# Attention scores in one burst over eight PSUM banks: one burst per pair, values per quad, FFN units in one stretch

## The chip, the cores and the metric

The kernel runs on one core of one Trainium2 chip. The metric is device time in microseconds, from runs of the whole kernel; lower is better. Before the change it takes 300.81 us (median of three runs, 300.67 to 305.9).

The engines are called by these names: PE (TensorE, the matrix multiplier), DVE (VectorE), ACT (ScalarE), POOL (GpSimd), SP (SyncE, which issues most DMAs). PSUM, into which PE writes its results, has eight banks of 512 fp32 columns on 128 partitions.

## What is computed

Attention with a causal mask over 576 tokens and 16 extra "beacon" keys that every query sees, for 8 batches of 8 heads of width 64; then a feed-forward layer (FFN) with the maximum of three projections over all 8 x 576 = 4608 tokens.

```python
k_all = np.concatenate([beacon_k, k], axis=2)          # (8, 8, 592, 64)
v_all = np.concatenate([beacon_v, v], axis=2)
scores = scale * np.matmul(q, k_all.transpose(0, 1, 3, 2))
scores = np.where(causal, -1000000000.0, scores)
a = np.exp(scores - scores.max(-1, keepdims=True))
a /= a.sum(-1, keepdims=True) + 1e-09
x = np.matmul(a, v_all)          # then (8, 576, 512) -> (4608, 512)
h = np.maximum(np.maximum(x @ w1, x @ w2), x @ w3)      # 512 -> 768
out = h @ w_out                                         # 768 -> 512
```

## The kernel before

Work is cut into *pairs* of heads (32: four per batch, numbered 0 to 31) and *quads* of two pairs (16). Keys of a pair lie in five tiles of 128 rows (the last has 80); tile t is needed by the queries from `q_min[t]` on (0, 112, 240, 368, 496). Everything is issued in an order written out by hand (`emit_all`, L834, under `manual_schedule`); no planner reorders it, and each engine runs its own list in order.

*Scores* (`emit_scores`, L438 to L460). The 1664 columns of a pair are split into four *groups* (`groups_any`, L69) of at most 512 columns. For each group PE multiplies the two heads of the pair side by side (64 rows of the array each) into two PSUM banks, one for each head (L450), and one ACT instruction exponentiates both into `at_sb` (L459). The pool `sc_psum` holds two such pairs of banks. POOL then zeroes the masked triangles (`emit_masks`, L478).

*Values* (`emit_pv`, L502 to L535). For a quad, four heads run side by side, 32 columns of the array each. Three parts are summed over the key tiles: a row of ones (the sums of the softmax), the even and the odd columns of V (L522). It is done in two halves of 288 queries, with two banks of the pool `pv_psum`. `invert_sums` (L538) takes Ln of the sums and Exp of minus that on ACT (L542, L544); `multiply` (L549, L554) has DVE multiply the values, read from PSUM, by it into `xT`, which holds four batches.

*FFN units*. A unit of `mm1_unit` (L572) is four matmuls of 512 columns (L582) into a bank of `ffn_psum` and one DVE copy (L590) or maximum (L592) into `hT`; one of `mm2_unit` (L613) is six matmuls (L618) and a DVE copy to `y` (L626), stored by SP (L652). A block of 512 tokens has 18 and 4 of them; there are nine blocks. `emit_ffn` (L674) emits the next unit if the running quota (`allowed`) and the finished batches (`ready`) permit.

*The order, from pair 4 on* (L844 to L893). Each pair has two steps of two groups: scores, masks, a half value pass of an earlier quad (in the first step), then FFN units and the other work of the step, with quota left over emitted at its end. "Turning" a pair is the transposing of its q and k by PE (L345) into PSUM and the copies to `qT` (ACT, L381) and `kT` (DVE, L392); it is done for pairs up to 15, one pair ahead. Pairs from 16 on are instead cast to bf16 by POOL (L218), stored to DRAM (L330) and fetched back by transposing DMAs (L337, L338), planned by `at_step` with pairs of lead. V is cast by POOL (L261). Loads are issued on SP as staging buffers come free.

*The end* (L895 to L908): the last quad's two halves between FFN units, and then FFN units alone, with the copies of the first projection given to ACT (`alone`) and banks taken from `ffn_psum` and `sc_psum` in turn.

Of the kernel before, what the change touches and what calls it, by code (L numbers as in the profile page):

```python
# [16 lines left out]
def kernel(  # L17
# [64 lines left out]

    def groups(p):
        return groups_0 if p < PPB else groups_any
# [8 lines left out]
    assert AT_W == g_base(PPB, NG)  # L93
    assert max(g_width(p, gi) for p in (0, PPB) for gi in range(NG)) <= 512
# [19 lines left out]
    at_pool = ctx.enter_context(tc.tile_pool(name="at", bufs=5))  # L114
    nrm_pool = ctx.enter_context(tc.tile_pool(name="nrm", bufs=2))
    ffn_h = ctx.enter_context(tc.tile_pool(name="ffn_h", bufs=2))
    ffn_y = ctx.enter_context(tc.tile_pool(name="ffn_y", bufs=5))
    sc_psum = ctx.enter_context(tc.tile_pool(name="sc_psum", bufs=2, space=PSUM))
    pv_psum = ctx.enter_context(tc.tile_pool(name="pv_psum", bufs=1, space=PSUM))
    dram_pool = ctx.enter_context(tc.tile_pool(name="dram", bufs=B - B_PE, space=bass.MemoryType.DRAM))  # L120
    ffn_psum = ctx.enter_context(tc.tile_pool(name="ffn_psum", bufs=2, space=PSUM))
# [32 lines left out]
    def pv_bank(i, shape, dtype):  # L154
        return pv_psum.tile(shape, dtype, name=f"pv{i}")
# [143 lines left out]
    def turn_beacons(b0, b1, src):  # L299
        n = Nb * (b1 - b0)  # L300
        ps = sc_psum.tile([128, PPB, n], BF16, name="sc")
        for pi in range(PPB):
            nc.tensor.transpose(
                ps[:, pi],
                src[:, 2 * pi : 2 * pi + 2].rearrange("p h d -> p (h d)"),
                ident[0:n, 0:n],
            )
        if b0 == 0:
            by_act(kTs[0][:, 0:Nb], ps[:, 0, 0:Nb])
        by_act(bT[:, :, Nb * b0 : Nb * b1], ps)  # L310
# [45 lines left out]
    def turn_half(p, h, pv, q_copy=None, idle=0):  # L356
        for i in range(2):
            src = stage.pop(("half16", p, h, i))
            if pv:
                bank = pv_bank(i, [128, 1024], BF16)  # L360
            else:
                bank = ffn_psum.tile([128, 1024], BF16, name="fps")
# [34 lines left out]
    def turn_apart(p, i):  # L397
        ps = ffn_psum.tile([128, S], BF16, name="fps")
        turn(p, i, ps)
        (evac_q, evac_k)[i](p, ps, by_dve)  # L400
        if i == 1:
            place_beacons(p, by_dve)

    def turn_pair(p, q_copy, shared=True):
        if shared:
            ps = sc_psum.tile([128, 2, 1024], BF16, name="sc")
            banks = [ps[:, i, 0:S] for i in range(2)]
        else:
            banks = [pv_bank(i, [128, 1024], BF16)[:, 0:S] for i in range(2)]
        for i in range(2):  # L410
            turn(p, i, banks[i])
        evac_k(p, banks[1], by_dve)
        evac_q(p, banks[0], q_copy)

    def keep_busy(n, cols=320, ffn=False):
        ps = ffn_psum.tile([128, 512], FP32, name="fps") if ffn else pv_bank(1, [128, 512], FP32)
# [23 lines left out]
    def emit_scores(p, gi):  # L440
# [4 lines left out]
        ps = sc_psum.tile([128, 2, 512], FP32, name="sc")  # L445
# [15 lines left out]
        )  # L461

# [35 lines left out]
    def emit_pv(quad, hf, first=0, last=len(passes), apart=False):  # L498
# [4 lines left out]
        if first == 0:  # L503
            if apart:
                banks = [ffn_psum.tile([128, 512], FP32, name="fps") for _ in range(2)]
            else:
                banks = [pv_bank(i, [128, 512], FP32) for i in range(2)]
# [27 lines left out]

    def invert_sums():
# [4 lines left out]
        lnd = nrm_pool.tile([128, HALF], FP32, name="lnd")  # L541
        nc.scalar.activation(out=lnd, in_=ps[0][:, 0:HALF], func=AF.Ln)  # L542
        recip = nrm_pool.tile([128, HALF], FP32, name="recip")
        nc.scalar.activation(out=recip, in_=lnd, func=AF.Exp, scale=-1.0)  # L544
# [26 lines left out]
    alone = [False]  # L571

    def mm1_unit(tb, ft, i, pool, name):
        if tb not in hTs:
            hTs[tb] = ffn_h.tile([128, n_ft, TOKB], BF16, name="hT")
        h = hTs[tb][:, ft]
        ps = pool.tile([128, TOKB], FP32, name=name)
        c0 = tb * TOKB % (RING * S)
        n0 = min(TOKB, RING * S - c0)
        for x0, o0, n in ((c0, 0, n0), (0, n0, TOKB - n0)):  # L580
            for ct in range(n_ct if n > 0 else 0):
                nc.tensor.matmul(  # L582
                    ps[:, o0 : o0 + n],
                    w_in[i][:, ct, 128 * ft : 128 * (ft + 1)],
                    xT[:, ct, x0 : x0 + n],
# [3 lines left out]
        if i == 0:  # L589
            (by_act if alone[0] else by_dve)(h, ps)  # L590
        else:
            nc.vector.tensor_max(h, h, ps)  # L592

    def mm1_halves(tb, ft, i, lo, hi, pool, name):
# [3 lines left out]
        ps = pool.tile([128, 2, MID], FP32, name=name)  # L598
# [14 lines left out]
    def mm2_unit(tb, tt, pool, name):  # L613
        hT = hTs[tb]
        c0 = tb * TOKB + 128 * tt
        ps = pool.tile([128, d_model], FP32, name=name)
        for ft in range(n_ft):
            nc.tensor.matmul(  # L618
                ps,
                hT[:, ft, 128 * tt : 128 * (tt + 1)],  # L620
                w_out_sb[:, ft, :],
                start=(ft == 0),
                stop=(ft == n_ft - 1),
            )
        y = ffn_y.tile([128, d_model], FP32, name="y")
        nc.vector.tensor_copy(y, ps)  # L626
        y_out.append((c0, y))

    def mm2_last(tb, tt, cuts):
# [3 lines left out]
        for i in range(len(cuts) - 1):  # L633
            lo, hi = cuts[i : i + 2]
            pool, name = ((ffn_psum, "fps"), (sc_psum, "sc"))[i % 2]
            ps = pool.tile([128, hi - lo], FP32, name=name)
# [33 lines left out]
    UPB = len(units) // n_tokb  # L670
    END = len(units)
    done = [0]

    def emit_ffn(limit, pool=None, name="fps"):  # L674
        if done[0] == len(units):
            return False
        need, fn, args = units[done[0]]
        if done[0] + 1 <= limit + 1e-6 and need <= ready[0]:
            fn(*args, pool or ffn_psum, name)
            done[0] += 1  # L680
            return True
        return False
# [136 lines left out]
    for quad in range(2, NPAIR // 2 - 1):  # L819
        at_pv(2 * quad + 2, 0, quad, 0)  # L820
        at_pv(2 * quad + 3, 0, quad, 1)
# [12 lines left out]
    def emit_all():  # L834
# [9 lines left out]
        for p in range(PPB, NPAIR):  # L844
            b, pi = divmod(p, PPB)
            turned = p + 1 < B_PE * PPB
            for s, gs in enumerate(steps(p)):
# [9 lines left out]
                if n_step <= N_FIRST:  # L857
                    allowed = first + n_step * (UPB - first) / N_FIRST
                else:
                    allowed = UPB + (n_step - N_FIRST) * UPB / (2 * PPB)  # L860
                if s == 0:
                    if p < PPB + 2:
                        turn_pair(p + 1, by_act, False)
                        emit_ffn(allowed)
                    elif p % 2 == 0:
                        emit_ffn(allowed)
                    if turned and p >= PPB + 2:
                        turn_pair(p + 1, by_act)
                    if p % 2 == 1 and p >= PPB + 2:
                        emit_ffn(allowed)  # L870
                    if turned:
                        place_beacons(p + 1, by_act)
# [4 lines left out]
                    emit_ffn(allowed, *(() if turned else (sc_psum, "sc")))  # L877
# [3 lines left out]
                else:  # L881
# [6 lines left out]
                    emit_ffn(allowed, *((sc_psum, "sc") if done[0] + 2 <= allowed else ()))  # L888
# [3 lines left out]
            if pi == 1 and b > 0:  # L892
                v_tiles.pop(b - 1)  # L893
        assert not plan and not loads and not pv_at
        for hf in range(2):  # L895
            multiply()
            emit_ffn(END)
            emit_ffn(END)
            emit_pv(NPAIR // 2 - 1, hf)
            finish_pv()  # L900
        store_y(len(y_out))
        alone[0] = True
        i = 0
        tail = [(ffn_psum, "fps"), (sc_psum, "sc")]
        while done[0] < END - 1 and emit_ffn(END, *tail[i % 2]):
            i += 1
# [35 lines left out]
```

## Time and profile before

| What | Before |
|---|---|
| Runs (median of three; lowest, highest) | 300.81 us (300.67, 305.9) |
| Span of the profiled execution | 299.3 us |
| Mean granted TensorE clock | 1.000 |
| PE busy | 282.3 us, 94% |
| DVE, ACT, POOL busy | 173.6, 145.8, 127.8 us |
| Exponentials (L459), 128 of them | 103.8 us |
| DMA moved | 50.68 MB |

The profiled execution's own total is not given apart from its span; the median of the runs is 1.5 us above the span.

The page of the profile gives, for each engine, busy time and its share of the span; then the span in 40 slices, each digit the busy share of a slice in tenths (PEclk is the clock granted to PE, in tenths of full). A line of a group of instructions reads: line of the kernel, engine, operation, output<-inputs, shapes, count, then busy time and mean length in ns, then the idle time of the engine just before these instructions and what ended it. A line of the timeline reads: start, length, engine, line, what, and how many; equal instructions that follow each other are merged. A line of the waits reads: who waited <- for whom: time in all, times, longest. Matmul ends are modelled, and a few matmul records are missing, so starts are the better measure on PE.

### The profile page before, as it was taken

What the parts mean: (1) busy time and instruction counts of PE and PEld (TensorE: products, weight loads), DVE (VectorE), ACT (ScalarE), POOL (GpSimd) and SP (SyncE); (2) the same over time, 40 slices, a digit from 0 to 9 for tenths busy, and PEclk for the clock granted to TensorE, in tenths of its full rate; (3) what the DMA queues carried; (4) which work ended last, traced back from release to release, by engine and by line L of the source; (5) the groups of instructions that cost most, each with busy time, mean ns of one, the idle gap of its engine ahead of it and who ended that gap; (6) DMA issues with size and microseconds to landing.
All of it is one profiled execution on the core that took longest, in us unless ns stands there. A gap on an engine that the chain in (4) does not pass through costs nothing.

```text
span 299.3 us, 8656 instructions
## 1 busy us (share of the span) xinstructions
PE 282.3 (94%) x3569; PEld 152.8 (51%) x3599; DVE 173.6 (58%) x346; ACT 145.8 (49%) x233; POOL 127.8 (43%) x253
## 2 busy tenths in 40 slices
PE   7879887999999999999999999999999999999994
PEld 4546654554545454454545777545454554444442
DVE  3756744555767575646563756375736575274372
ACT  3685484875665465546453646364636421401300
POOL 7181776666475674456455635552333210000000
PEclk9999999999999999999999999999999999999999
DMA  8989999999999999899989999894111002103003
GB/s 147 197 161 235 226 211 265 239 224 296 241 268 209 200 289 220 168 189 330 231 165 204 287 260 189 144 257 103 42 72 70 2 2 85 57 1 140 2 0 142
DMA packets 85320, 50.68 MB, mean 169 GB/s; under 512 B 64416, under 2 KB 80032, under 8 KB 85280
## 3 DMA queue, kind: packets, MB, share of 16 engines
q1 hardware_dynamic: 80672, 45.76, 67.4%
q0 software_dynamic: 4048, 4.03, 8.2%
q8 instruction: 28, 0.46, 0.7%
q10 hardware_dynamic: 560, 0.33, 0.5%
q14 instruction: 12, 0.10, 0.1%
HBM read 35.13 MB, written 14.22 MB: 165 GB/s over the span
## 4 chain that ended last, share of the span: by engine, by line
PE 81%; DMA 7%; SPq 4%; DVE 2%; ACT 2%; issue 1%; POOL 1%; POOLq 0%; DVEq 0%
PE fps L582 31%; PE sc L582 12%; PE pv L522 11%; PE fps L618 11%; PE sc L450 8%; DMA st<-in_k_dram 4%; PE sc L618 4%; SPq L245 3%; DMA quad<-in_k_dram 3%; PE sc L345 2%; ACT at_sb L459 1%; DVE xT L554 1%; POOL quad L209 1%; DVE y L626 1%; PE fps L522 0%
## 5 line engine op out<-in xcount | busy, mean ns | idle before, releaser
L459 ACT ACTIVATE at_sb<-sc 128x928 bf16<-128x928 f32 (+5 forms) x128 | 103.8, 861 | 85.2 <-PE sc L450 84.7
L582 PE MATMUL fps<-xT,w_sb 128*128 128x512 bf16 (+1 forms) x464 | 106.4, 356 | 2.1 <-issue 0.8
L478 POOL TENSOR_SCALAR_AFFINE_SELECT at_sb<-at_sb 128x256 bf16<-128x256 bf16 (+2 forms) x148 | 53.8, 382 | 99.0 <-ACT at_sb L459 98.8
L582 PEld LDWEIGHTS <-w_sb 128*128 128x128 bf16 x672 | 61.7, 98 | 65.2 <-issue 12.2
L592 DVE TENSOR_TENSOR hT<-hT,fps 128x512 bf16<-128x512 bf16 x70 | 48.0, 687 | 29.4 <-PE fps L582 29.1
L218 POOL CAST p<-st 96x768 bf16<-96x768 f32 x56 | 44.6, 822 | 1.0 <-DMA st<-in_k_dram 0.5
L582 PE MATMUL sc<-xT,w_sb 128*128 128x512 bf16 (+1 forms) x187 | 42.9, 356 | 0.1
L450 PE MATMUL sc<-qT,kT 64*128 64x288 bf16 (+5 forms) x400 | 36.0, 277 | 2.8 <-ACT at_sb L459 1.9
L618 PE MATMUL fps<-w_out_sb,hT 128*128 128x512 bf16 x143 | 34.6, 379 | 0.9 <-issue 0.6
L618 PEld LDWEIGHTS <-hT 128*128 128x128 bf16 x210 | 19.8, 98 | 24.1 <-DVE hT L592 2.1
L592 DVE TENSOR_TENSOR hT<-hT,sc 128x512 bf16<-128x512 bf16 x32 | 22.0, 688 | 16.9 <-PE sc L582 11.3
L626 DVE COPY y<-fps 128x512 f32<-128x512 f32 x25 | 17.3, 692 | 23.5 <-PE fps L618 23.5
L590 DVE CAST hT<-fps 128x512 bf16<-128x512 f32 x32 | 22.1, 692 | 12.3 <-PE fps L582 12.2
L554 DVE TENSOR_TENSOR xT<-pv,recip 128x288 bf16<-128x288 f32 (+2 forms) x93 | 27.3, 349 | 2.7 <-ACT recip L544 2.7
L522 PE MATMUL pv<-at_sb,v_sb 128*32 128x288 bf16 (+5 forms) x1376 | 28.7, 229 | 0.0
L450 PEld LDWEIGHTS <-kT 64*128 64x128 bf16 x400 | 14.3, 94 | 27.2 <-issue 21.8
L522 PEld LDWEIGHTS <-v_sb 128*32 128x32 bf16 (+1 forms) x1408 | 24.4, 96 | 1.9 <-issue 0.6
L261 POOL CAST v_sb<-st 128x1536 bf16<-128x1536 f32 (+2 forms) x21 | 18.4, 893 | 1.8 <-DMA st<-in_v_dram 1.8
L522 PE MATMUL pv<-at_sb,ones 128*32 128x288 bf16 (+4 forms) x500 | 17.4, 256 | 1.3 <-POOL at_sb L478 1.2
L542 ACT ACTIVATE lnd<-pv 128x288 f32<-128x288 f32 x31 | 12.9, 417 | 8.9 <-PE pv L522 8.9
L522 PEld LDWEIGHTS <-ones 128*32 128x32 bf16 (+2 forms) x512 | 10.9, 95 | 8.7 <-issue 6.7
L590 ACT CAST hT<-sc 128x512 bf16<-128x512 f32 x6 | 3.5, 585 | 23.7 <-PE sc L582 23.7
(74 smaller groups left out, 161.7 us busy)
## 6 DMA issues: line engine op xcount, KB each, us to landing
out_dram<-y SPq DMA_DIRECT2D x35, 256.0 KB, 3.5
st<-in_q_dram SPq DMA_DIRECT2D x28, 288.0 KB, 5.6
st<-in_k_dram SPq DMA_DIRECT2D x28, 288.0 KB, 6.2
st<-in_v_dram SPq DMA_DIRECT2D x24, 256.0 KB, 6.0
w_sb<-in_moe_w_dram POOLq DMA_DIRECT2D x6, 384.0 KB, 7.2
q_dram<-p SPq DMA_DIRECT2D x16, 144.0 KB, 2.4
k_dram<-p SPq DMA_DIRECT2D x16, 144.0 KB, 2.9
st<-in_v_dram SPq DMA_DIRECT2D x8, 224.0 KB, 6.1
```

Source lines behind the costliest of these rows:

```text
L218: cast(t16.rearrange("p r h d -> p h r d"), st[0:QP, i * NQ2 : (i + 1) * NQ2].rearrange("p (h r d) -> p h r d", h=2, r=QR),)
L261: cast(v_sb[0:n, t:t1].rearrange("p t h d -> p (t h d)"), st[0:n, (t - t_lo) * H * D : (t1 - t_lo) * H * D],)
L450: nc.tensor.matmul(ps[:, e, off : off + q1 - q0], kT[hs, 128 * t : 128 * t + 128], qT[hs, q0:q1], start=True, stop=True, tile_position=(64 ...
L459: nc.scalar.activation(out=both_heads(p, gi), in_=ps[:, :, 0 : g_width(p, gi)], func=AF.Exp, scale=scale)
L478: nc.gpsimd.affine_select(out=view, in_=view, compare_op=ALU.is_ge, fill=0.0, base=x0, pattern=[[0, 2], [1, hi - lo]], channel_multiplier=-1,)
L522: nc.tensor.matmul(ps[bank][32 * j : 32 * j + 32, lo + q0 - qa : lo + qb - qa], lhsT, at_view(PPQ * quad + j // 2, t, j % 2, q0, qb), star ...
L554: nc.vector.tensor_mul(xT[:, 2 * g + part - 1, c0 + ca : c0 + cb], ps[bank][:, lo : lo + cb - ca], recip[:, ca:cb],)
L582: nc.tensor.matmul(ps[:, o0 : o0 + n], w_in[i][:, ct, 128 * ft : 128 * (ft + 1)], xT[:, ct, x0 : x0 + n], start=(ct == 0), stop=(ct == n_c ...
L590: (by_act if alone[0] else by_dve)(h, ps)
L592: nc.vector.tensor_max(h, h, ps)
L618: nc.tensor.matmul(ps, hT[:, ft, 128 * tt : 128 * (tt + 1)], w_out_sb[:, ft, :], start=(ft == 0), stop=(ft == n_ft - 1),)
L626: nc.vector.tensor_copy(y, ps)
```

## The change

Three things change from pair 8 on (`FIRST_BURST`, batch 2), and PSUM is one tile of eight banks, `acc`, instead of three pools. For the pairs before, `Banks` hands out fixed banks as the pools did.

- *One score burst per pair*: the four groups, cut anew (`groups_whole`, from pair 6 on), are multiplied one after another into eight banks that are handed out in turn (`next_bank`); each group's exponential reads its two banks in one strided view. The cut has groups of 208, 464, 496 and 496 columns for each head.
- *One value burst per quad*: `emit_pv_whole` takes all 576 queries at once, 496 of them in one bank for each of the three parts and the last 80 of all three in a fourth bank, directly after the burst of the next even pair. ACT copies the values to SBUF (`raw`), then does Ln and Exp; DVE multiplies `raw` by the result at the end of the pair (`finish`).
- *FFN units of a pair in one stretch*, each in the next bank in turn; the last unit of a stretch is done in two halves of 256 columns in two banks (`close`). Turning comes after the first unit, planned work after the second and at the end.

`at_pool` has 4 buffers instead of 5. The pairs 4 to 7 keep their order, but no longer take FFN banks from the score pool, and pair 6 turns before its first FFN unit. At the end, the last quad's values come in one burst after three FFN units, all banks go in turn, and DVE does the copies that ACT did (`alone` is gone).

```diff
+    groups_whole = [
+        [(3, q_min[3], S)],
+        [(1, q_min[1], S)],
+        [(0, 0, TAIL)],
+        [(2, q_min[2], S), (0, TAIL, S), (4, q_min[4], S)],
+    ]
...
-    at_pool = ctx.enter_context(tc.tile_pool(name="at", bufs=5))
+    at_pool = ctx.enter_context(tc.tile_pool(name="at", bufs=4))
...
+    acc = psum.tile([128, N_BANK, 512], FP32, name="acc")
...
+    free_banks = list(range(N_BANK))
+
+    def next_bank():
+        i = free_banks.pop(0)
+        free_banks.append(i)
+        return i
...
+    def emit_burst(p):
+        at[p] = at_pool.tile([128, AT_W], BF16, name="at_sb")
+        for gi in range(NG):
+            lo, hi = sorted(next_bank() for _ in range(2))
+            off = 0
+            for t, q0, q1 in groups(p)[gi]:
+                for e in range(2):
+                    score(p, t, e, q0, q1, acc[:, (lo, hi)[e], off : off + q1 - q0])
+                off += q1 - q0
+            nc.scalar.activation(
+                out=both_heads(p, gi),
+                in_=acc[:, lo : hi + 1 : hi - lo, 0 : g_width(p, gi)],
+                func=AF.Exp,
+                scale=scale,
+            )
...
+    def emit_pv_whole(quad):
...
+        banks = [next_bank() for _ in range(4)]
+        runs = [(part, banks[part], 0, 0, TAIL) for part in range(3)]
+        runs += [(part, banks[3], part * WT, TAIL, S) for part in range(3)]
...
+        raw = pv_pool.tile([128, 2, S], FP32, name="raw")
+        for part in (1, 2):
+            nc.scalar.copy(raw[:, part - 1, 0:TAIL], acc[:, banks[part], 0:TAIL])
+        nc.scalar.copy(
+            raw[:, :, TAIL:S],
+            acc[:, banks[3], WT : 3 * WT].rearrange("p (i c) -> p i c", i=2),
+        )
+        recip = nrm_pool.tile([128, S], FP32, name="recip")
+        nc.scalar.activation(out=recip[:, 0:TAIL], in_=acc[:, banks[0], 0:TAIL], func=AF.Ln)
+        nc.scalar.activation(out=recip[:, TAIL:S], in_=acc[:, banks[3], 0:WT], func=AF.Ln)
+        nc.scalar.activation(out=recip, in_=recip, func=AF.Exp, scale=-1.0)
+
+        def finish():
+            c0 = b % RING * S
+            for i in range(2):
+                nc.vector.tensor_mul(xT[:, 2 * g + i, c0 : c0 + S], raw[:, i], recip)
...
+        for p in range(FIRST_BURST, NPAIR):
+            b, pi = divmod(p, PPB)
+            emit_burst(p)
+            finish = emit_pv_whole(p // 2 - 1) if p % 2 == 0 else None
+            for gi in range(NG):
+                emit_masks(p, gi)
...
+            while may_emit(allowed):
+                n_y = len(y_out)
+                emit_ffn(allowed, next_psum, not may_emit(allowed, 1))
+                store_y(n_y)
+                n += 1
+                if n == 1 and p + 1 < B_PE * PPB:
+                    turn_pair(p + 1, by_act, "any")
+                    place_beacons(p + 1, by_act)
+                if n == 2:
+                    for fn in plan.pop((p, 0), ()):
+                        fn()
+            if finish:
+                finish()
+            for s in range(2):
+                for fn in plan.pop((p, s), ()):
+                    fn()
```

## The prediction

> **What bounds the kernel now.** Read the page first: span, busy shares, slices.
>
> ```profile
> span 299.3 us, 8656 instructions
> PE 282.3 (94%) x3569; PEld 152.8 (51%) x3599; DVE 173.6 (58%) x346; ACT 145.8 (49%) x233; POOL 127.8 (43%) x253
> PE   7879887999999999999999999999999999999994
> PEclk9999999999999999999999999999999999999999
> ```
>
> TensorE (PE) is the bound: after slice 8 (60 us) it is full, at full clock, while VectorE (DVE), ScalarE (ACT) and GpSimd (POOL) have half their time free. Next, the table of waits: of what PE waits for, the largest is
>
> ```profile
> PE sc L450 <- ACT at_sb L459: 1.9, 5, 0.9
> ```
>
> and the five fall before 60 us. So where the change starts (pair 8, 64.3 us), PE has no waits to lose; a gain must come out of its own stream, and any wait added is paid in full. The PE timeline of a pair late in the kernel:
>
> ```profile
> 195.68 1.03 PE L582 MATMUL fps<-xT,w_sb 128*128 128x512 bf16 x4
> 196.64 0.54 PE L450 MATMUL sc<-qT,kT 64*128 64x288 bf16 x8
> 197.12 0.40 PE L522 MATMUL pv<-at_sb,ones 128*32 128x288 bf16 x12
> 197.35 0.62 PE L522 MATMUL pv<-at_sb,v_sb 128*32 128x288 bf16 x32
> 198.78 1.03 PE L582 MATMUL sc<-xT,w_sb 128*128 128x512 bf16 x4
> 199.64 1.03 PE L582 MATMUL fps<-xT,w_sb 128*128 128x512 bf16 x4
> 200.60 0.51 PE L450 MATMUL sc<-qT,kT 64*128 64x464 bf16 x4
> 201.05 1.04 PE L582 MATMUL fps<-xT,w_sb 128*128 128x512 bf16 x4
> ```
>
> Starts count, not durations (each includes some 165 ns of pipeline that the next matmul overlaps). An FFN unit of four 512-column matmuls takes 199.64 − 198.78 = 0.86 us, 216 ns a matmul, 0.42 ns a column. From 195.68, four such end at 196.54, but the scores start at 196.64: 0.10 is lost. From 200.60, 464 + 336 columns (two heads side by side) are 0.34, but the FFN starts 0.45 later: 0.11 lost. The starts of single matmuls between 60 and 245 us give the loss at each change of tile shape with hardly any scatter: 96 ns FFN to scores, 92 scores to FFN, 90 scores to values, 96 values to FFN. That is what the change can save.
>
> Last, the exponentials, by form and from the ACT timeline:
>
> ```profile
> L459 ACT ACTIVATE at_sb<-sc 128x992 bf16<-128x992 f32 x32 | 31.9, 997 | 36.5 <-PE sc L450 35.9 <-POOL at_sb L478 0.5
> L459 ACT ACTIVATE at_sb<-sc 128x928 bf16<-128x928 f32 x28 | 26.4, 944 | 45.2 <-PE sc L450 45.2
> L459 ACT ACTIVATE at_sb<-sc 128x672 bf16<-128x672 f32 x28 | 20.3, 726 | 0.0
> 56.78 3.16 ACT L459 ACTIVATE at_sb<-sc 128x928 bf16<-128x928 f32 x4 [0.50 <-PE sc L450]
> ```
>
> Four in a row, one pair's worth, take 3.16 us, while a pair's score matmuls take 0.7. Today a step's scores are followed by work in other banks, and no one waits for the exponentials.
>
> **The change, part by part.** Sums are against the profiled execution (span 299.3); the median of the runs, 300.81, lies 1.5 above it (launch and end), which I add back.
>
> *Removed: changes of shape.* Pairs 8 to 31 are 24. Before, each has two score steps (48 entries, 48 exits) and one half value pass with an exit of its own (24); the last quad's two halves add 4: 124. After: 24 + 24 + 12 + 2 = 62. Saved 62 × 94 ns = **−5.8 us**. The columns stay: scores 1664 a pair both ways; value burst, from starts of groups of four (288: 122 ns, 192: 82, 96: 42, 80: 40, 48: 27), 2.18 us a quad before in 120 matmuls and 2.20 after in 108: +0.3 in all.
>
> *Added: waits of PE for exponentials.* A burst takes banks in turn from eight, in pairs, one pair a group, and goes round all eight. One exponential reads both banks of its group as a strided view `acc[:, lo : hi+1 : hi-lo]`. If a burst starts at an even bank the groups are (0,1), (2,3).. If it starts at an odd bank, one group is (7,0), sorted to lo 0, hi 7. The view touches two banks, but its first and last address enclose all eight, and in the built program the next write of *any* bank waits for that exponential. An example from the built order is pair 13, where the banks run 3,4 / 5,6 / 7,0 / 1,2: the 496 columns go to banks 0 and 7, and the first write of bank 1 then carries a wait for ScalarE, at the count of the exponential of banks 0 and 7:
>
> ```
> L510 Matmult acc_90<-qT1_109,kT1_115 128x496
> L510 Matmult acc_90<-qT1_109,kT1_115 128x336 [waits Activation_49]
> ```
>
> Start banks follow from the counts (8 for scores, 4 for values on even pairs, one per FFN unit and one more for the split last one, 2 for a turn). Odd starts: pairs 10, 17, 22 (bank 1: group 3 wraps), 13, 14, 21, 26 (bank 3: group 2), 25, 30 (bank 5: group 1), 18, 29 (bank 7: group 0). Eleven of 24.
>
> Price, from the burst's first score: group 0 is 208 columns wide, so its exponential (416 elements, 0.51 by the slope 997 to 726 over 320 elements, 0.85 ns each) starts at about 0.32 and ends at 0.83; each later one adds its length less 0.105 of overlap (3.16 against 3.45 summed): ends 0.83, 1.67, 2.56, 3.45. PE resumes 52 ns after the exponential that it waits for (51 to 52 ns at each of the five waits above, by single starts). Unhindered, PE would start group 1 at 0.09, group 2 at 0.30, group 3 at 0.51, the next kind of work at 0.82. So wrap at group 3: 3.50 − 0.82 = 2.69, three times 8.1; group 2: 2.61 − 0.51 = 2.10, four times 8.4; group 1: 1.72 − 0.30 = 1.43, twice 2.9; group 0: 0.88 − 0.09 = 0.79, twice 1.6. Sum **+20.9 us**, nothing else on PE being late enough to absorb it. Bounds: 0, if they were all hidden; 27 if ScalarE began each chain 0.5 later. I take the worked value, for ScalarE is idle at a burst's start (below). Behind the waiting matmul stand all of PE's queue: the rest of the burst, the value burst, the FFN; DVE's evictions and POOL's masks follow late but are not the bound.
>
> *Ordinary bursts (13).* The next work takes group 0's banks: 0.88 against 0.82, 0.06 each; group 3's second bank waits for the last half eviction about as long, and the two overlap: **+0.9**.
>
> *Split last unit.* Eight 256-column matmuls (109 ns by starts) for four of 216: +8 ns, 24 times, +0.2. Where that unit is the first output unit right after the last maximum (pairs 12, 16, 20, 24, 28), its sixth matmul comes at 0.55, and the eviction that it needs ends at 0.19 + 0.69 + 0.05 = 0.93: 0.39 × 5 = **+1.9**. Bounds 0 and 3.
>
> *ScalarE copies values, VectorE multiplies from SBUF.* Per quad ACT gains copies of 496 twice (0.57 each, between 585 for 512 and 425 for 320) and 160 (0.3), and has Ln 0.59 + 0.24 and Exp 0.69 for four of 0.42 to 0.44. In an even pair that ends with the copy of qT (0.64) near 6.6, the pair is over 8.5 long: hidden, and free at the next burst. The sums' bank comes free at 5.1 against an FFN unit that wants it at 5.5: hidden by 0.4; without this cover, 0.5 × 12 = 6. DVE: 576 columns from SBUF, no row; from 450 at 288 and 248 at 96, 0.75, twice per quad; DVE has 42% free, and they run behind the pair's last eviction, before the next pair's first unit ends. Hidden.
>
> *Moved: casts, stores, fetches.* Per pair two pair casts on POOL, two stores and two transposing fetches on SP, and per batch the three V casts and the loads that they release, go behind the pair's second FFN unit or its end. A fetch lands 3 to 5 us after issue and is used over two pairs (16 us) later, on SP's queue behind output stores that wait only for an earlier unit. POOL takes masks first, then casts. The second V cast is now needed with the first value tiles: after masks (to 4.5), cast 1.46, pair casts 1.6 and 0.6 it is done near 8.2 after the odd pair's burst; the burst needs it near 8.3. Value 0, bounds 0 and 6 × 0.7. Pairs 4 to 7 lose the spare score banks for FFN units, and pair 6 turns before its unit: 0, bounds ±1. At the end VectorE takes ScalarE's 12 copies (692 ns each, unit 0.86): hidden.
>
> Sum: 299.3 − 5.8 + 0.3 + 20.9 + 0.9 + 0.2 + 1.9 = 317.7; plus 1.5: **319 us**, 6% slower.
>
> **Rivals.** (1) *Not slower*: the wrapped waits cost nothing because the exponentials are done when PE arrives. Then 319.2 − 20.9 = 298.3. It decides if the eleven waits come to under 2.5 us in all (8.5 for less than 2% slower); for it speaks only ScalarE's 51% idle time, against it that a pair's exponentials cannot finish before 3.1 us after its scores began. Chance 0.08; a further 0.02 for this without the smaller costs (295.0) and with some saving that I do not see, below 294.8. (2) *ScalarE or the V cast is late*, so each chain begins some 0.25 later: 24 × 0.25 = 6, **325**. For: in even pairs with a turn ScalarE's list ends only 2 us before the burst. Against: 2 us is spare. 0.14. (3) *The clock falls in the gaps.* The profile never shows it below full in gaps up to 1.2 us; it fell 4.1 us after the last matmul (295.2 to 299.3), and the start took 4.4 us at half speed. Up to 2.2 us lost in each of the three long waits: **326**. The gaps of 2.7 are nearer to the 4.1 that drops it than to 1.2, but short of it: 0.05. (4) *The wrapped waits are shorter*, say group 3's and 2's cut by a third through earlier starts: 319 − 5.5 = 313.5. 0.08.
>
> On rival 3: the Trainium skill, "TensorE: Matmul & The Clock Gate", section "Why this matters for your kernels", asks for no idle gaps over about 3 us between bursts of matmuls, since the clock then halves. By it the 2.7 us gaps still pass and the sum stays; a longer one would not. The trace agrees as far as it goes: full clock through every gap below 1.2 us, and a drop after 4.1.
>
> **How the numbers follow.** Forecast 319 (0.63); rivals 0.10, 0.14, 0.05, 0.08. Range 310 to 326: rival 4 and a cheaper chain below, rivals 2 and 3 above; rival 1 is left out. Within 2% of 300.8 (what a measurement here tells from no change) lie 294.8 to 306.8: rival 1 but for its 0.02. Faster 0.02, same 0.08, slower 0.90.
>
> **What would show it.** In the profile after: PE waits for the exponential's line from score lines, value lines and FFN lines, eleven times 0.8 to 2.7 us, some 21 us in all, at pairs 10, 13, 14, 17, 18, 21, 22, 25, 26, 29, 30, and nothing longer than 0.1 at the others; PE busy share down to about 89%; 62 fewer shape changes. Wrong if those waits are absent, or if PE waits for VectorE, POOL or a DMA instead.

## The result, and the profile after

The changed kernel takes 326.07 us (median of 4 runs, 325.05 to 328.76) against 303.36 for the kernel before (4 runs, 300.67 to 307.42) beside it: 1.0806 times the time, 95% interval 1.0711 to 1.0901. It is slower by about 8%. 319.0 was forecast, with a range of 310 to 326: the sign was right, and the time lies just above the range. Medians here are of all runs, while ratios and their intervals leave out the runs in a slower state, which the kernel before and most others show now and then. The profiled execution of the changed kernel took 325.05 us, with a span of 323.3.

The page of the profile after, with the span, the busy shares, the slices of TensorE (PE) and of its clock, and the groups of the exponentials and of the new operations:

```profile
span 323.3 us, 8611 instructions
PE 288.2 (89%) x3539; PEld 165.1 (51%) x3539; DVE 182.0 (56%) x330; ACT 150.0 (46%) x247; POOL 132.9 (41%) x253
PE   7789969996997979968997889987998899999995
PEclk9999989997999899979998999999999999999999
L528 ACT ACTIVATE at_sb<-acc 128x416 bf16<-128x416 f32 (+1 forms) x96 | 76.1, 867 | 87.1 <-PE acc L510 56.1
L651 DVE TENSOR_TENSOR xT<-raw,recip 128x576 bf16<-128x576 f32 x26 | 20.7, 838 | 0.0
```

PE falls from 94% to 89% of the span, and its row now has sixes, sevens and eights where it was all nines from 60 us on. The row below it is the one to look at a second time: the clock, all nines before, now dips five times. Nothing else is nearer to its limit than it was.

The table of waits of the changed kernel (who waited <- for whom: time in all, times, longest):

```profile
PE acc L510 <- ACT at_sb L528: 12.5, 8, 2.0
PE acc L628 <- ACT at_sb L528: 5.0, 2, 2.5
PE acc L750 <- ACT at_sb L528: 2.6, 1, 2.6
...
PE acc L750 <- DVE hT L722: 1.4, 5, 0.3
```

Eight, two and one: the eleven waits for ScalarE (ACT), met by score lines (L510), by value lines (L628) and by an FFN line (L750), as forecast. By the starts of single matmuls they are 2.60, 2.72 and 2.68 us at pairs 10, 17 and 22, 2.14 or 2.15 at 13, 14, 21 and 26, 1.46 and 1.47 at 25 and 30, 1.18 and 1.12 at 18 and 29: 21.8, or 21.5 without the change of shape (some 93 ns) that the first three contain. PE resumes 51 to 54 ns after the exponential's end. One more wait, of 0.77 us, falls on pair 8 itself, whose first burst waits for pair 7's last exponential; the kernel before lost 0.39 and 0.18 in that pair.

One of them, and what follows it, in the PE timeline of the changed kernel (pair 17: 12 score matmuls from 138.11, then FFN), and in its table of stretches (us; busy time and instructions of each engine; then granted clock, DMA share, GB/s):

```profile
138.11 0.97 PE L510 MATMUL acc<-qT,kT 64*128 64x208 bf16 x12
141.65 4.65 PE L750 MATMUL acc<-w_out_sb,hT 128*128 128x512 bf16 x13 [2.56 <-ACT at_sb L528]
```

```profile
135.00:138.45 3.45, 3.16 (x25) 1.77 (x24) 2.50 (x5) 0.00 (x0) 0.00 (x0) 1.00 1.02 133
138.45:141.86 3.41, 0.85 (x11) 0.47 (x8) 1.73 (x3) 3.13 (x4) 1.66 (x4) 1.00 0.70 171
141.86:145.27 3.41, 3.41 (x10) 1.17 (x9) 0.69 (x1) 0.00 (x0) 3.41 (x6) 0.50 0.64 171
145.27:148.70 3.43, 3.43 (x20) 1.84 (x19) 1.80 (x3) 0.00 (x0) 1.14 (x3) 1.00 0.80 239
```

In the second stretch PE is busy for 0.85 of 3.41 us; in the third the granted clock is 0.50, and in the fourth it is 1.00 again. So the wait is paid twice: once as a gap, and once at half speed behind it. From pair 8 on there are four such stretches, at 77.01, 104.32, 141.86 and 176.00 us, each 3.413 long, and all whole multiples of 3.413 apart. A stretch of 3.413 at half speed does 1.71 less of work: 6.8 us in all, in this execution. The other three runs had mean clocks of 0.968, 0.973 and 0.951 against its 0.973, so the number of falls is not the same in each.

**Where the time went.** The stretch from the first score of pair 8 to PE's last matmul is the measure for all that follows: 237.2 us in the kernel before (57.79 to 294.99), 260.7 after, 23.5 longer. What lies before pair 8 (the head) differs between executions of one kernel: pair 8 begins at 59.8 us in one profile of e2 below and at 62.9 in the other.

| term | us |
|---|---|
| eleven waits for the exponentials | +21.5 |
| four stretches at half clock | +6.8 |
| second-product halves waiting for hT, 0.40 once and 0.46 four times | +2.2 |
| last group's second bank (below, e8 and e9), and the split unit | +2.3 |
| pair 8's own burst, 0.77 against 0.39 and 0.18 | +0.2 |
| 62 fewer changes of shape at 94 ns | -5.8 |
| small stalls of the kernel before that are gone (hT 0.41, three of 0.33 for xT, some 1.3 in the FFN) | about -2.7 |
| sum / measured | 24.5 / 23.5 |

The 1.0 us between sum and measurement is not assigned.

### The profile page after: what moved, and what is told of

Same layout as the page of the kernel before. It is cut to its first block, busy times and chain, and to the rows that moved or that the text cites. A ratio compares the mean times of both kernels' runs of the same rounds, so it can differ in the third digit from the quotient of the medians.

```text
span 323.3 us, 8611 instructions
## 1 busy us (share of the span) xinstructions
PE 288.2 (89%) x3539; PEld 165.1 (51%) x3539; DVE 182.0 (56%) x330; ACT 150.0 (46%) x247; POOL 132.9 (41%) x253
## 4 chain that ended last, share of the span: by engine, by line
PE 73%; ACT 9%; DMA 6%; POOL 4%; issue 3%; DVE 3%; SPq 1%; ACTq 0%; POOLq 0%; DVEq 0%
PE acc L703 39%; PE acc L750 13%; PE acc L628 10%; ACT at_sb L528 7%; PE acc L510 5%; DMA st<-in_v_dram 3%; DMA quad<-in_k_dram 2%; ACT at_sb L504 2%; POOL v_sb L303 2%; PE acc L387 1%; PE acc L594 1%; DVE hT L722 1%; POOL p L260 1%; PE acc L495 1%; SPq L222 1%
## 5 line engine op out<-in xcount | busy, mean ns | idle before, releaser
L703 PE MATMUL acc<-xT,w_sb 128*128 128x512 bf16 (+1 forms) x732 | 136.5, 342 | 0.0
L528 ACT ACTIVATE at_sb<-acc 128x416 bf16<-128x416 f32 (+1 forms) x96 | 76.1, 867 | 87.1 <-PE acc L510 56.1
L703 PEld LDWEIGHTS <-w_sb 128*128 128x128 bf16 x732 | 69.8, 98 | 57.8 <-issue 0.8
L722 DVE TENSOR_TENSOR hT<-hT,acc 128x512 bf16<-128x512 bf16 (+1 forms) x114 | 69.8, 630 | 38.7 <-PE acc L703 36.1
L750 PE MATMUL acc<-w_out_sb,hT 128*128 128x512 bf16 (+1 forms) x246 | 53.4, 369 | 4.0 <-ACT at_sb L528 2.6
L720 DVE CAST hT<-acc 128x512 bf16<-128x512 f32 (+1 forms) x54 | 33.0, 630 | 41.5 <-PE acc L703 35.3
L757 DVE COPY y<-acc 128x512 f32<-128x512 f32 (+1 forms) x41 | 25.1, 613 | 31.6 <-PE acc L750 16.3
L750 PEld LDWEIGHTS <-hT 128*128 128x128 bf16 x246 | 24.0, 102 | 29.0 <-issue 7.7
L510 PE MATMUL acc<-qT,kT 64*128 64x80 bf16 (+4 forms) x288 | 25.1, 282 | 13.1 <-ACT at_sb L528 12.5
L504 ACT ACTIVATE at_sb<-acc 128x992 bf16<-128x992 f32 (+6 forms) x32 | 26.3, 863 | 13.1 <-PE acc L495 13.0
L510 PEld LDWEIGHTS <-kT 64*128 64x128 bf16 x288 | 12.8, 94 | 27.4 <-issue 22.2
L628 PE MATMUL acc<-at_sb,v_sb 128*32 128x80 bf16 (+5 forms) x936 | 24.2, 249 | 0.0
L651 DVE TENSOR_TENSOR xT<-raw,recip 128x576 bf16<-128x576 f32 x26 | 20.7, 838 | 0.0
L628 PE MATMUL acc<-at_sb,ones 128*32 128x80 bf16 (+5 forms) x468 | 14.2, 248 | 5.0 <-ACT at_sb L528 5.0
L628 PEld LDWEIGHTS <-v_sb 128*32 128x32 bf16 (+1 forms) x936 | 16.2, 100 | 4.3 <-issue 0.2
```

What stands on the lines that cost most here:

```text
L504: nc.scalar.activation(out=both_heads(p, gi), in_=ps[:, :, 0 : g_width(p, gi)], func=AF.Exp, scale=scale)
L510: nc.tensor.matmul(ps, kTs[p % NT][hs, 128 * t : 128 * t + 128], qTs[p % NT][hs, q0:q1], start=True, stop=True, tile_position=(64 * e, 0),)
L528: nc.scalar.activation(out=both_heads(p, gi), in_=acc[:, lo : hi + 1 : hi - lo, 0 : g_width(p, gi)], func=AF.Exp, scale=scale,)
L628: nc.tensor.matmul(acc[32 * j : 32 * j + 32, bank, lo + q0 - qa : lo + qb - qa], lhsT, at_view(PPQ * quad + j // 2, t, j % 2, q0, qb), sta ...
L703: nc.tensor.matmul(ps[:, a:b], w_in[i][:, ct, 128 * ft : 128 * (ft + 1)], xT[:, ct, x0 : x0 + b - a], start=(ct == 0), stop=(ct == n_ct - 1),)
L720: by_dve(h[:, lo:hi], ps[:, lo:hi])
```

## The experiments

Each kernel stands beside runs of the kernel before on the same chip: 303.45 us (median of 23) for e1 to e4, 301.65 (19) for e5 to e8, 304.71 (17) for e9 and the two repeats.

**e1_two_exps.** The exponential whose banks are 7 and 0 is written as two, one for each bank, so that no view encloses the others.

```diff
-            nc.scalar.activation(
-                out=both_heads(p, gi),
-                in_=acc[:, lo : hi + 1 : hi - lo, 0 : g_width(p, gi)],
...
+            for e0, e1 in ((0, 1), (1, 2)) if hi - lo > 1 else ((0, 2),):
+                nc.scalar.activation(
+                    out=both_heads(p, gi)[:, e0:e1],
+                    in_=acc[:, (lo, hi)[e0] : (lo, hi)[e1 - 1] + 1, 0 : g_width(p, gi)],
```

> The changed kernel, but where a group's banks are 0 and 7 its exponential is done as two instructions, one for each bank, so that no view spans the banks between; nothing else differs. Theory A (the eleven waits for a view over banks 0 and 7 cost 21.5 us, and the clock drops that these gaps bring cost 6.8): span 323.3 - 21.5 - 6.8 + 0.7 (eleven ordinary bursts' waits of 0.06) = 295.7, time near 297.5, clock 0.99 or more from pair 8 on. Rival B (bursts themselves are dear: PE waits for a chain of four exponentials, ScalarE or VectorE is late): still over 310.

Measured: 301.29 us, 0.9975 of the kernel before (0.9935 to 1.0015). From pair 8 to the last matmul 233.9 us, 26.8 less than the changed kernel, with no half-speed stretch in it. One more instruction in eleven of 24 bursts takes all of the slowdown away. The 297.5 us expected was not reached: the stretch is within 1 us of theory A (260.7 - 21.5 - 6.8 + 0.7 = 233.1), but pair 8 began at 66.1 us in this profile, the longest of the twelve runs, against 58.7 in the changed kernel's.

**e2_even_start.** Where the stretch of FFN units would end on an odd bank, a bank is passed over, so that every burst starts on an even one and no group has banks 7 and 0.

```diff
-                emit_ffn(allowed, next_psum, not may_emit(allowed, 1))
+                last = not may_emit(allowed, 1)
+                while last and not (free_banks[2] % 2 == 0):
+                    next_bank()
+                emit_ffn(allowed, next_psum, last)
```

> The changed kernel, but before the split last unit of a pair one bank is left out when that is needed for the next burst to begin at an even bank; no group then gets banks 0 and 7. No instruction is added. Theory A: as with two exponentials, near 297.5, no wait over 0.2 us at any burst. Rival B: over 310. Rival C (the two further exponentials matter): differs from the kernel with two exponentials by more than 1 us.

Measured: 299.77 us, 0.9928 (0.9885 to 0.9972). From pair 8 on 233.95, as e1 to 0.05, by another way. The medians of e1 and e2 differ by 1.5 us, more than rival C's 1, but in the profiles the difference lies before pair 8, where e1 and e2 are the same code. In the table of its waits the 11 for L528 are gone and the halves' five are left; two of its rows:

```profile
PE acc L495 <- ACT at_sb L504: 2.1, 5, 0.9
...
PE acc L750 <- DVE hT L722: 1.4, 5, 0.3
```

So the strided view over banks 0 and 7 is the cause of the waits, and the rest of the change is worth 237.2 - 233.95 = 3.3 us. The 26.7 us that e2 takes off are the 21.5 and the 6.8, less 1.5 by which the last group's second matmul, no longer covered by a long wait, comes later in sum. The same kernel again (**e2_again**) took 301.22, 0.9887 (0.9841 to 0.9932), and 233.87 from pair 8 on.

> The kernel of e2_even_start again, beside e5 and e9 on the same chip: by the stretch from pair 8 to TensorE's last matmul (234.0 us here, 232.7 in e5), e5 is 1.3 us faster; medians also hold what the clock did before pair 8, so they may differ from that by some 2 us. 299.8.

**e3_all_group0, e4_all_group3 and e6_all_group2.** As e2, but the bank that the burst starts on is fixed at 7, 1 or 3 (`free_banks[2] == 7`, `1`, `3`): then each of the 23 bursts from pair 9 on, not eleven, has the enclosing view, always in the same group. Short gaps, long ones, and those in between.

> The changed kernel, with banks left out before a pair's last unit so that every burst from pair 9 on begins at bank 7: group 0, the first, has banks 0 and 7 in 23 bursts. Theory A: 23 waits of about 1.15 us (the two of this kind in the changed kernel took 1.18 and 1.12), 26 us in all, and, gaps being short, a clock near 1.0: span 295.7 + 26 = 322, time near 324. If clock drops do not hang on the length of a gap (rival D), mean clock near 0.97 as in the changed kernel and 7 us more, 331.

> As before it, but every burst from pair 9 on begins at bank 1: group 3, the last, has banks 0 and 7 in 23 bursts. Theory A: 23 waits of about 2.65 us, 61 us. The clock (drops at the end of a 3.413 us window, on a grid, when PE was idle for some 2 us of it): a gap of 2.65 meets that at about 6 phases in 10, 14 drops of 1.7 us, 24 us: span about 381, clock about 0.94. Without clock drops (rival D) 357.

> As e3_all_group0 and e4_all_group3, with banks so set that the pair 0 and 7 always falls to group 2, whose wait was 2.14 us in the changed kernel. 23 waits, some 2.1 us each: 48 us on the 297.7 us span of e2, 346 without any fall of the clock. Theory A (the clock halves for one window of 3.413 us where TensorE stood still for about 2.0 us or more of the window of 3.413 us before it): a gap of 2.14 us does so only where it lies whole in one window, 37% of places, so 6 to 11 windows x 1.7 us = 10 to 19 us more: 356 to 365 span, 358 to 367. Rival B (the length of the gap decides, and 2.14 us is too short, as the 1.1 us gaps of e3 are): no half-speed windows behind pair 8, 348. Rival C (every gap over 2 us does): 23 windows, 385.

Measured: e3 324.87 us, e4 390.79, e6 365.06; ratios 1.0758 (1.0676 to 1.0841), 1.2941 (1.2834 to 1.3048), 1.2132 (1.2065 to 1.2199). Their largest waits and mean clocks, one fence for each kernel and view, in the order e3, e6, e4:

```profile
PE acc L510 <- ACT at_sb L528: 23.0, 23, 1.1
```

```profile
core 0: 323.4 us, clock 0.983
```

```profile
PE acc L510 <- ACT at_sb L528: 45.9, 23, 2.0
```

```profile
core 0: 362.4 us, clock 0.939
```

```profile
PE acc L628 <- ACT at_sb L528: 27.9, 11, 2.5
PE acc L750 <- ACT at_sb L528: 15.3, 6, 2.6
PE acc L703 <- ACT at_sb L528: 15.0, 6, 2.5
```

```profile
core 0: 387.8 us, clock 0.910
```

e3 waits for ScalarE in all as long as the changed kernel does (23.0 against 20.1 in these rows), yet its clock falls in the head only and not once from pair 8 on; its 324.87 us are within 1 us of the 324 expected. e6 has 10 half-speed stretches there, e4 has 18, where 14 and a span of 381 us were expected: four more at 1.7 us are the 6.8 by which its 387.8 is longer. Total waiting does not decide, and neither does the length of a gap alone: in e6 23 gaps, all 2.1 us long, led to 10 falls. The tables of stretches of e6 and, in the last two lines, of the changed kernel, cut at the 3.413 us that the falls keep to, show what does:

```profile
148.07:151.49 3.42, 3.13 (x21) 1.74 (x19) 2.46 (x5) 0.00 (x0) 0.00 (x0) 1.00 0.77 194
151.49:154.90 3.41, 1.43 (x16) 0.68 (x15) 2.10 (x4) 2.32 (x4) 1.47 (x3) 1.00 0.24 84
154.90:158.31 3.41, 3.41 (x9) 1.21 (x8) 0.69 (x1) 0.92 (x1) 2.43 (x4) 0.50 0.00 0
202.69:206.10 3.41, 1.53 (x15) 0.89 (x13) 1.35 (x3) 2.16 (x3) 1.87 (x4) 1.00 1.15 264
206.10:209.51 3.41, 3.27 (x121) 2.56 (x121) 0.00 (x0) 2.73 (x6) 2.16 (x5) 1.00 0.93 280
```

```profile
172.59:176.00 3.41, 1.53 (x13) 0.89 (x14) 2.39 (x4) 2.19 (x3) 1.08 (x2) 1.00 0.83 197
176.00:179.41 3.41, 3.31 (x13) 1.34 (x13) 0.00 (x0) 1.05 (x2) 1.99 (x4) 0.50 0.33 101
```

In e6 a stretch with 1.43 us of busy PE is followed by half speed; one with 1.53 is not. The gap was as long in both (2.14 and 2.18 by starts), but in the second its last 0.14 lay in the stretch behind, which has 3.27 busy of 3.41. At the border the busy time of the tables does not separate the cases: in the changed kernel a stretch with 1.53 did bring a fall. Better are the starts of single matmuls, with gaps no longer than a change of shape left out. Over all 298 stretches of the changed kernel and of e3, e4 and e6 from pair 8 on there are 32 falls, each behind a stretch with 1.94 to 2.78 us of idle PE; no stretch with more than 2.06 passed without one, and none below 1.94 brought one. With the short gaps counted too, the falls begin at 2.05 and one stretch with 2.14 passes. So the limit is near 2.0 of 3.413 us, known to some 0.1. Theory A of e6 named 6 to 11 stretches and 358 to 367 us, and got 10 and 365.06.

**e5_whole_mm2.** e2, and the last unit of a pair is split only if it belongs to the first product.

```diff
                 last = not may_emit(allowed, 1)
-                while last and not (free_banks[2] % 2 == 0):
+                close = last and units[done[0]][1] is mm1_unit
+                while last and not (free_banks[1 + close] % 2 == 0):
                     next_bank()
-                emit_ffn(allowed, next_psum, last)
+                emit_ffn(allowed, next_psum, close)
```

> The fixed banks of e2_even_start, and the last unit of a pair is computed in halves only where it is a first-product unit; where it is a second-product unit (pairs 12, 16, 20, 24, 28) it stays whole. What stood in the trace of e2 are five waits of 0.46 us of a second-product half for the copy of the first-product unit just before it. Theory A (the wait comes from cutting the unit and so bringing the consumer 1.3 us nearer its producer's copy): no, the producer is the unit before in either case, so the wait stays and the time is that of e2, 299.8. Theory B (a whole second-product unit starts with matmuls that need only the earlier rows of hT, and reaches the late one last; cut in halves, the first half reaches it after half the time): the waits shrink to under 0.1 us each, 2.2 us less, 297.5. B follows from the order of the six matmuls over ft and is the one held.

Measured: the five waits for hT are gone, as theory B has it; from pair 8 on 232.69 us, 1.3 less than e2 and not 2.2. The rest went to a later place: a whole unit's bank is copied out later, and the last score group of the burst, whose second matmul takes that bank, starts that matmul 0.34 to 0.41 us behind its first there, where e2 has 0.08 to 0.15. The median was 302.22 us, 0.9948 (0.9894 to 1.0001), above e2's, so the time of the whole program did not show the gain. Its repeat beside e2, **e5_again**:

> The kernel of e5_whole_mm2 again, beside e2 and e9 on the same chip: 1.3 us under e2 by the stretch from pair 8 on, 298.5, if the 302.2 of the first time was the clock before pair 8 (six of its eight times lay at 302 or above, two at 297.6 and 298.9); the same 302 again if the kernel itself brings that on.

301.52 us, 0.9834 (0.9769 to 0.9900), and 232.68 from pair 8 on, against 301.22 and 233.87 for e2 beside it. Of the first eight times of e5 five, not six, lay at 302 or above; of the six here two lay near 298 and four at 301.4 or above, so that it comes in two groups is seen again, and why is not shown. The medians do not tell e2 and e5 apart; the stretch does, to 0.1 us in both repeats. Pair 8 began at 59.2 us in the one profiled run of e5 and at 63.7 in the other.

**e7_no_raw.** e2 without the copies by ScalarE: VectorE (DVE) multiplies straight from PSUM, at once.

```diff
-        raw = pv_pool.tile([128, 2, S], FP32, name="raw")
-        for part in (1, 2):
-            nc.scalar.copy(raw[:, part - 1, 0:TAIL], acc[:, banks[part], 0:TAIL])
...
+        for i in range(2):
+            nc.vector.tensor_mul(
+                xT[:, 2 * g + i, c0 : c0 + TAIL],
+                acc[:, banks[1 + i], 0:TAIL],
+                recip[:, 0:TAIL],
+            )
```

> The fixed banks of e2_even_start, without ScalarE's copies of the values: VectorE multiplies straight out of PSUM, at once behind the inversion and ahead of the pair's FFN evictions. Theory A (ScalarE's copies are hidden, as the prediction costed them at nothing, and so is their absence): ScalarE loses some 14 us of work, TensorE's order is unchanged, time within 1 us of e2, 299 to 301. Theory B (what the copies buy is that VectorE does not stand still for the inversion): VectorE's evictions queue behind multiplies that wait some 2 to 3 us for the reciprocal and then take about 2.6 us, the second-product units that follow a late hT wait, up to 2 us on each of 12 quads: 303 to 323. Held: A at 0.5, B at 0.5 with the low end likelier.

Measured: 314.38 us, 1.0469 (1.0414 to 1.0524); from pair 8 on 246.1, 12.2 more than e2. Theory B. The DVE timeline of e7, and one row of its waits:

```profile
160.94 1.25 DVE L641 TENSOR_TENSOR xT<-acc,recip 128x496 bf16<-128x496 f32 x2 [4.27 <-ACT recip L638]
162.11 0.38 DVE L647 TENSOR_TENSOR xT<-acc,recip 128x80 bf16<-128x80 f32 x2
162.41 3.06 DVE L724 TENSOR_TENSOR hT<-hT,acc 128x512 bf16<-128x512 bf16 x5
```

```profile
PE acc L752 <- DVE hT L724: 6.1, 18, 1.1
```

DVE stands still for 4.27 us until the reciprocal is there, and five evictions stand behind it in DVE's queue; the second-product halves that follow then wait for three of them (164.34, 164.93 and 165.53 us), and so in five pairs (18 such waits in all). In six more pairs the next burst's scores wait, 0.2 us each in the table and 0.4 by starts. The copies cost nothing, as the prediction said, but they are not idle: they let DVE put the multiplies off to the end of the pair.

**e8_unit_in_burst.** e2, and one FFN unit of each pair goes between the second and the third score group.

```diff
+            if gi == 1:
+                middle()
...
+            def middle():
+                if may_emit(allowed, 2):
+                    emit_ffn(allowed, next_psum)
+                    next_bank()
```

> The fixed banks of e2_even_start, and one FFN unit of every pair from 8 on is put between the second and the third score group: 24 more stretches of scores and as many more of FFN, with the same matmuls in sum. Theory A (each change of the shape of the tile costs TensorE 90 to 97 ns, which is the 5.8 us that the change saves): 48 more changes x 94 ns = 4.5 us more than e2, 304.3. Rival B (the gain of the change came from fewer ordinary waits and not from the shape changes): within 1 us of e2, 299 to 301.

Measured: 302.22 us, 1.0050 (1.0015 to 1.0084); from pair 8 on 235.40, only 1.45 more than e2. By single starts each of the 24 new entries into scores costs 96 ns and each exit 93, 4.5 us as theory A has it. But 3.1 came back: the second matmul of the last group (336 columns), which starts some 0.13 us late in e2's bursts, is on time in e8 (3 or 4 ns behind the first).

**e9_long_groups_first.** Is that because its bank was the last FFN unit's? e5, with the 208-column group last.

```diff
-        return groups_any if p < FIRST_WHOLE else groups_whole
+        if p < FIRST_WHOLE:
+            return groups_any
+        return groups_whole if p < FIRST_BURST else groups_whole[1:] + groups_whole[:1]
```

> e5_whole_mm2 with the four score groups of the bursts in another order from pair 8 on: 464, 496, 336+80+80, 208 columns instead of 208, 464, 496, 336+80+80. In the traces of e2 and e5 the second matmul of the last group starts some 0.13 us late in almost every burst, and later still (0.2 to 0.4) where the last FFN unit is a whole second-product unit; e8, where that group comes with an FFN unit shortly before it on other banks, does not have it. Theory A (the last group's second bank is the one that the last FFN unit wrote, and VectorE has not copied it out yet): the group now starts 0.12 us later in the burst, at 0.62 instead of 0.50, so most of the loss goes, 2 to 3 us over 24 bursts: 2 to 3 us less than e5 in the same call. Rival B (TensorE's instructions come late at the end of a burst of 24 short ones): the last group is late as before, whichever it is: the time of e5.

Measured: 313.75 us, 1.0282 (1.0226 to 1.0337): 10.6 more than e5 from pair 8 on, where 2 to 3 less was expected. The late second matmul did go: the last group's is on time, or up to 0.08 late, in most pairs, and 0.22 to 0.29 late where a whole second-product unit ended the stretch, so theory A holds for it. The changed kernel's trace shows the same at single starts: in pairs 11 and 12 VectorE's copy of the last half ends 0.58 us after the burst's first score, and the late matmul starts 54 ns behind that. But a wait came that I had not worked out. From the PE timeline and the waits of e9:

```profile
185.75 0.93 PE L512 MATMUL acc<-qT,kT 64*128 64x464 bf16 x12
187.24 4.53 PE L705 MATMUL acc<-xT,w_sb 128*128 128x256 bf16 x40 [0.56 <-ACT at_sb L530]
```

```profile
PE acc L630 <- ACT at_sb L530: 6.3, 11, 0.6
PE acc L705 <- ACT at_sb L530: 3.5, 6, 0.6
PE acc L752 <- ACT at_sb L530: 2.2, 6, 0.4
```

After the burst the next work takes the first group's banks. With 208 columns first, that exponential ends just as the burst does (0.88 against 0.82 by the prediction's working); with 464 first it starts and ends later, and every burst waits up to 0.6 us. With eight banks in turn, the order of the groups is held from both ends: the shortest first, for the banks taken next, and the last as late as can be, for the bank just filled.

## Why the prediction was wrong, point by point

**The failed step: the clock.** Rival 3 was right in kind ("the clock falls in the gaps") and had 0.05, as gaps of 2.7 us were held short of the 4.1 that dropped it in the kernel before; nothing of it was in the sum. It happened four times, 6.8 us, against the 6.05 by which the profiled execution is above 319; e1 and e2, without the gaps, have none from pair 8 on; e6 has 10 and e4 18. Without the 6.8 the span would have been 316.5, where the sum gave 317.7; that this is so near is in part luck, for some 2 us of waits put too low and 2.7 us of stalls that went unnoticed offset each other. What misled me was comparing the length of a gap with a limit. The 4.1 us after the last matmul was no limit either: counted back by 3.413 from the fall at 299.31, the stretch before ended at 295.90 and had been busy until 295.24, so by the same rule the next place for a fall was 299.31. The rule that the rows obey is a share of a stretch of fixed place: about 2.0 idle of 3.413 us. By it, even 2.14 us is enough if it lies whole within one stretch, and one of 2.68 (pair 22) passes where the cut falls inside it. Rival 3 also priced only the three longest waits, at up to 2.2 us each; the falls came after pairs 10, 13, 17 and 21, that is, after two long ones and two of 2.14 us, at 1.7 each. The rule that the prediction weighed, of the Trainium skill, "TensorE: Matmul & The Clock Gate", section "Why this matters for your kernels" (no idle gaps over about 3 us), would have let all these gaps pass; the trace contradicts it, with falls behind gaps of 2.14 to 2.72 us. The same page of the Trainium skill, in "Part 1: The HAM clock gate", tells of a free-running window of 3413 ns; the 3.413 us between falls agree with that, and I had not used it.

**The eleven waits: right.** Pairs, groups and order as worked out from the banks; 21.5 us against 20.9. Groups 1 and 2 came within 0.05 of 1.43 and 2.10; group 3's three, without the change of shape in them, were 2.51 to 2.63 against 2.69. Group 0 was 1.12 and 1.18 and not 0.79, and the trace shows why: the enclosing view made the exponential itself late. It started 0.65 and 0.70 us after the burst's first score and not 0.32, both times 115 to 116 ns behind the end of VectorE's copy of the last FFN half, from a bank that it does not read; all 23 of e3 do the same, while group 0's exponentials that read neighbouring banks (pairs 11, 20 and 25, for example) started at 0.35 to 0.37. So the view was tied to other engines' use of the banks between in both directions: it waited for them, and they for it.

**Changes of shape: right.** 124 to 62, at 88 to 98 ns each in both kernels, and again in e8. What was missed is that the kernel before also had some 2.7 us of small stalls from pair 8 on that the change removes, where the prediction had "no waits to lose".

**Ordinary bursts, 0.9: too small.** The wait for group 3's second bank was named there, at about 0.06 each and overlapping. It is some 0.09 a pair in the changed kernel, 2.1 in all, and about 3 us in e2, where no longer wait covers it. e8 and e9 show which bank it is.

**Split units, 1.9: right.** 2.2 measured, in the pairs named; e5 shows that the split itself brings them, and that 0.9 of their price moves elsewhere when it is left out.

**ScalarE's copies and the moved work at nothing: right.** No wait on V casts, on pair casts or on `raw` from pair 8 on; so rival 2 is out, and e7 shows that without the copies it would have been 12 us slower. VectorE's multiply takes 838 ns where 0.75 us was worked out, and is hidden.

**Rivals 1 and 4.** Out: no wait was shorter than worked out by more than 0.18. A slip in the text: pair 8 begins at 57.79 us in the kernel before (64.3 is pair 9), so the last of the five waits, 0.2 us at 58.40, lies in the part that changed; no term hung on it.

What the change could have been worth: e2 and e5 are below the kernel before by 0.5 to 1.7% (the four ratios above; one of the intervals reaches 1.0001), and 3.3 and 4.5 us shorter from pair 8 on. What stays open is the head. In the profiles of the changed kernel and its variants the clock falls there once or twice, for 3.4 to 20.5 us, in that of the kernel before it does not, and pair 8 begins anywhere from 57.8 to 66.1 us; nothing was tried there.

## What to carry to other kernels

Where buffers are handed out in turn, look at each view that takes the last and the first together: a dependence is kept for all that lies between, for those who wait for the view and for the view itself, and with eleven such views one kernel lost 21 us in waits that e1 removed with a second instruction. Price a wait of the bound engine twice: as the gap, and as what the clock does behind it, by adding up the idle time in each stretch of the clock's own grid and not by the length of the gap. When the order in a burst is changed, ask for both ends at once who takes the first buffer next and who filled the last one.

## What the runs showed of the hardware

- The granted clock of TensorE changed only at places a whole number of times 3.413 us apart within one run. The places are not the same from run to run: counted from the span's start they lie at 1.92 us and whole multiples of 3.413 on in the changed kernel's profile, 1.54 in e3's, 1.30 in e6's and 0.91 in e4's. In 32 cases of four kernels it fell to 0.50 for one such stretch after a stretch with 1.94 us or more of idle time, and it never fell after one with less; from 2.07 on it always did. Between, both occur.
- A fall lasts exactly one stretch if the matmuls go on at once, as in all 32 cases. In the head, where gaps follow each other, it lasted 6.83 us in e1, e3, e6, e7, e8 and e9, 13.65 us in e9 and in the repeat of e5, and 20.48 in the repeat of e2.
- From pair 8 on the kernels repeat to 0.1 us (e2: 233.95 and 233.87; e5: 232.69 and 232.68) while whole runs scatter by 4 to 7 us. In the two pairs of profiles the spans differ by 3.0 and 4.5 us, all of it before pair 8; of the runs that were not profiled this is not shown. To compare variants, the length of a stretch that both have says more than the medians.
